# Attention then mixer on one core: 128-row blocks of keys, 23 pairs by DMA transposes, another seed

## The chip, the core and the metric

The kernel runs on one core of a Trainium2 chip. A core has a matrix engine (TensorE, PE in the profile, with its weight loads as PEld), a vector engine (VectorE, DVE), a scalar engine (ScalarE, ACT), a general engine (GpSimd, POOL) and an engine that here issues all DMAs (SyncE, SP). They run side by side and meet through semaphores. The metric is the device time of one execution in microseconds; lower is better. Before the change it is 1030.91 us, the median of three runs (1030.42 to 1031.17).

## The reference

Eight batches of eight heads, 576 positions, 64 channels a head. Attention is causal by blocks of 64 positions; its output is mixed along the sequence with two thin matrices and along the channels with a two-layer network.

```python
def _attn_ref(q, k, v):
    scores = scale * np.matmul(q, k.transpose(0, 1, 3, 2))
    mask = block_i >= block_j                  # blocks of 64 positions
    scores = np.where(mask, scores, -1000000000.0)
    scores = scores - np.max(scores, axis=-1, keepdims=True)
    attn = np.exp(scores)
    attn = attn / (np.sum(attn, axis=-1, keepdims=True) + 1e-09)
    return np.matmul(attn, v)

def _moe_ref(x, U, V, w_ch1, w_ch2):           # x: (8, 576, 512)
    h = x.transpose(0, 2, 1) @ U @ V           # U: (576, 32), V: (32, 576)
    u = x + h.transpose(0, 2, 1)
    ch = np.maximum(u @ w_ch1, 0.0) @ w_ch2    # 512 -> 2048 -> 512
    return u + ch
```

## The kernel before

The 64 heads are worked on in 32 pairs, four pairs to a batch. The 576 queries of a head fall into five tiles: tile 0 has the first 64 queries, and tile i has queries 128 i - 64 to 128 i + 64. Because of the mask tile i needs the first 128 i + 64 keys: i whole blocks of 128 keys and one odd block of 64.

For each pair `scores` multiplies q and k on TensorE (line 1323) in two sets, VectorE takes the maxima (line 1351), and ScalarE the exponentials (line 1362). One set's PSUM banks must be read before the next set's scores start. What follows has two forms. Up to pair 10 the probabilities stay in 32 bits: GpSimd divides them (line 1383), TensorE transposes them (line 1537), ScalarE and VectorE copy the transposes out of PSUM (lines 1508 and 1510), and `apply_v` multiplies them with v in 32 bits (line 1558). The pairs in `XP`, 11 to 31, split each probability into two 16-bit halves (`halve`, lines 1413 to 1440). The DMA engines transpose the halves, four transposes to a pair, issued by SyncE (line 1449), and `apply_x` multiplies them with the two halves of v (line 1487): three products of 16-bit halves for each block.

In `apply_x` the transposed blocks of tiles 0, 3 and 4 lie in one set of buffers (the profile calls them pw or spare) and those of tiles 1 and 2 in another (turn). From pair 24 on there is one set of the first for one pair; before, there are two. The columns of tile 4 are rotated by 64, so that its odd block shares a block of 128 rows with the odd blocks of tiles 0 and 3. In that block v has zeros in rows 0 to 63. The odd blocks of tiles 1 and 2 are followed by zeros, written once at the start (memsets after line 1200, columns 320 to 383 and 576 to 639 of the second buffer). The products go in two groups with a PSUM bank each: group 1 (tiles 3, 4), then group 0 (tiles 0, 1, 2). Odd blocks are read with 64 rows but for tile 4's, which is read with 128. ScalarE moves each bank out (line 1502), and `mix` takes the result through U and V (lines 1587 to 1667) and writes u to DRAM.

Each batch then has two chunks of 288 tokens in the mixer's first half (`ffn_chunk`, lines 763 and 788, chunks 0 to 15), which needs the scale of the whole batch. The second half (`block_products`, line 1012) runs after the attention, since its buffers take the attention's place. Its weights are prepared by ScalarE, VectorE and GpSimd (line 865, among others).

The order of the work is made when the program is built: a planner simulates the five engines with a cost for each task, and gives an engine that is free the ready task of the lowest priority number. Attention tasks have numbers up to 64,000; the mixer's products on TensorE have 1,000,000 and more, so they fill holes. `VARIANT` is the seed of a disturbance of up to 2% either way on every planned cost. SyncE, too, works in the planned order.

Of the kernel before, what the change touches and what calls it, by code (L numbers as in the profile page):

```python
# [18 lines left out]
P = 128  # L19
# [39 lines left out]
INTO = {"PE": 355, "DVE": 60, "ACT": 60, "POOL": 200, "SP": 60}  # L59
NEAR, DL, PORT = 130, 3000, 200  # L60
MOVES, AHEAD, LAND = 400, 1500, 2000
VARIANT = 50
PEQ = 1450.0
PVX = 150.0
NF = 6
# [11 lines left out]
KP = 1  # L77
START = {"PE": 4400, "DVE": 3100, "ACT": 2400, "POOL": 2700, "SP": 700}
SPL = 5
XP = tuple(range(11, 32))  # L80
SLOTS = (8, 5)
XS, XD, MOVE = 1400.0, 3500, 3000
XG = (2, 3)
# [114 lines left out]
class Plan:  # L198
# [8 lines left out]
    def add(self, engine, ns, prio, fn, reads=(), writes=(), hold=(), after=0, port=False, move=410):  # L207

        n = len(self.tasks)
        ns *= 1 + 0.04 * ((n * 40503 + 7919 * VARIANT) % 65536 / 65536 - 0.5)  # L210
        deps = set()
        for b in reads:
            deps.update(b.writers)
            if b.pool is not None:
                deps.update(m for m in b.readers if self.tasks[m][0] != engine)
            b.readers.append(n)
        for b in hold:
            deps.update(b.readers, b.writers)
        for b in writes:
            deps.update(b.readers, b.writers)  # L220
            b.writers, b.readers = [n], []
        deps.discard(n)
        slots = [b for b in dict.fromkeys((*reads, *writes)) if b.pool is not None]
        for b in slots:
            b.users += 1
        self.tasks.append((engine, ns, prio, fn, deps, after, slots, port or engine == "POOL", move))
# [116 lines left out]
def attention_then_mixer(  # L343
# [32 lines left out]
    def buf(pool, shape, dtype, name):  # L376
        return Buf(pool.tile(shape, dtype, name=name))
# [29 lines left out]
    def take(r, name):  # L407
        n = used[name] = used.get(name, -1) + 1
        return r[n % len(r)]
# [68 lines left out]
    def largest(src, n, buf, mu, i, prio):  # L478

        add(  # L480
            "DVE", _dve(n), prio,
            lambda: nc.vector.tensor_reduce(out=mu[:, i : i + 1], in_=src(), op=ALU.max, axis=AX.X, apply_absolute_value=True), [buf], [mu.parts[i]],
        )
# [36 lines left out]
    def power_of(mu, sc, prio, pool):  # L520

        row, ba = take(row_r[1], "rowv"), Buf(pool=pool)
        add(
            "PE", 115, prio,
            lambda: nc.tensor.transpose(out=ba[:, 0:P], in_=mu[:, 0:1].to_broadcast([P, P]), identity=factor["ident"].ap),
            [mu.parts[0]], [ba],
        )

        def exponent():
            x = row[:, 0:1]  # L530
            nc.vector.tensor_reduce(out=x, in_=ba[:, 0:P], op=ALU.max, axis=AX.X)
            nc.vector.tensor_scalar(out=x, in0=x, scalar1=TINY, scalar2=2.0 ** -22, op0=ALU.max, op1=ALU.mult)
            for n, op in enumerate((ALU.bitwise_xor, ALU.bitwise_and)):
                last = nc.vector.tensor_scalar(
                    out=sc[:, n : n + 1].bitcast(I32), in0=x.bitcast(I32), scalar1=EXPONENT, scalar2=EXPONENT,
                    op0=ALU.bitwise_and, op1=op,
                )
            return last

        add("DVE", 730, prio, exponent, [ba], [row, sc])  # L540
# [658 lines left out]
    def turn_of(h, g):  # L1199
        if g:  # L1200
            x = turn_lo[h // 2 % 2][h % 2]
            return x[:, : 2 * SLOTS[1], :], [x]
        x = pw_of(h)[1]
        return x.ap.bitcast(F16)[:, : 2 * SLOTS[0] * P].rearrange("p (a q) -> p a q", q=P), x.parts

    vh = buf(ep, [P, 10, D], F16, "vh")
# [72 lines left out]
    def load_v(p, pr):  # L1279
# [5 lines left out]
        )  # L1285
        if p in XP:
            add("POOL", 250, pr, lambda: nc.gpsimd.memset(raw[0:64, 4:10:5, :], 0.0), [], [raw])

    def job(p):

        if p in XP:
            return ((0, 4), (1, 3), (0, 0), (0, 1), (1, 2))
# [4 lines left out]
    def scores(p, s, pr):  # L1297
# [8 lines left out]
        def view(i):  # L1306
            rows, w = P if i else 64, P * i + 64
            if i == 4:
                return wide[:, :, :T]
            if i > 1:  # L1310
                return pair[i - 2][:, :w]
            return wide[:rows, side[i][0], side[i][1] : side[i][1] + w]

        def products(mine):

            def block(x, n, k0=0, k1=None):
                r = slice(64 * x, 64 * x + 64)
                i, c = (n + 1) // 2, 64 * (n > 0 and n % 2 == 0)
                k1 = 64 * (n + 1) if k1 is None else k1
                at = (k0 + 64) % S if i == 4 and p in XP else k0  # L1320
                o = view(i)[c : c + 64]
                o = o[:, at // T, at % T : at % T + k1 - k0] if i == 4 else o[:, k0:k1]
                nc.tensor.matmul(o, raw[r, 64 * n : 64 * n + 64], raw[r, S + k0 : S + k1], start=True, stop=True)  # L1323

            for x in mine:
                block(*x)
# [7 lines left out]
        else:  # L1334
            if p == XP[0] and not s:
                add("DVE", 130, pr, lambda: nc.vector.memset(wide[0:64, 0, 0:64], NEG), [raw], [wide], hold=[before[-2]])
# [3 lines left out]
                lambda: products((  # L1340
                    *(last if p in XP else ((a, 7, 0, T), (a, 8, 0, T), (b, 5), (b, 6), (a, 7, T, 512), (a, 8, T, S))),
                    (b, 3), (b, 4), (a, 1), (a, 2), (a, 0),
# [110 lines left out]
    def apply_x(p, pr):  # L1453
        xt, vr = xt_r[p % 2], vr_r[p % 2]
        vl = vr.ap.rearrange("p a b -> p (a b)").bitcast(F16).rearrange("p (a b x) -> p a b x", b=D, x=2)[:, :, :, 0]
        turned = [[turn_of(2 * p + s, g) for g in range(2)] for s in range(2)]
        sc, mu = take(vs_r, "vs"), take(mv_r, "mv")
        largest(lambda: vr.ap.rearrange("p a b -> p (a b)"), 10 * D, vr, mu, 0, pr)
        power_of(mu, sc, pr, banks_p(p))
        iv = sc[:, 1:2]  # L1460
        add(
            "POOL", 145 + 0.85 * 10 * D, pr,
            lambda: nc.gpsimd.tensor_scalar(
                out=vr.ap, in0=vr.ap, scalar1=sc[:, 0:1], scalar2=2.0 ** -16, op0=ALU.mult, op1=ALU.mult
            ),
            [sc], [vr],
        )
        add("ACT", _act(10 * D, True), pr, lambda: nc.scalar.copy(vh.ap, vr.ap), [vr], [vh])
        add("POOL", 60 + 2.2 * 10 * D, pr, lambda: nc.gpsimd.tensor_sub(vl, vr.ap, vh.ap), [vh], [vr])
        bank = [Buf(pool=banks_p(p)) for _ in range(2)]  # L1470
        n = [QS[g + 1] - QS[g] for g in range(2)]
        whole = [vh, vr, *(b for r in turned for _, x in r for b in x)]
        order = Buf()

        def products(g):
            for i in ((0, 1, 2), (3, 4))[g]:
                t, at, _ = slot_of[i]
                own, at = i in (3, 2), -(-at // P)
                half = 3 if i == 4 else at + i
                ops = [(j, v, a) for j in range(i + 1) for v, a in ((vh.ap, 0), (vl, 0), (vh.ap, 1))]  # L1480
                for m, (j, v, a) in enumerate(ops):
                    w = P if j < i else 64
                    x = max(P * i + 64 - QS[g] - w, 0)
                    o = 64 if i and w == 64 else 0
                    r = slice(0, P if j < i or i == 4 else 64)
                    for s in range(2):
                        nc.tensor.matmul(  # L1487
                            bank[g][64 * s : 64 * s + 64, x : x + w], v[r, 5 * s + j, :],
                            turned[s ^ own][t][0][r, SLOTS[t] * a + (at + j if j < i else half), o : o + w],
                            start=m == 0, stop=m == len(ops) - 1,  # L1490
                        )

        for g in (1, 0):
            cost = 3 * sum(2 * i + 4 + 0.425 * (P * i + 64) for i in ((0, 1, 2), (3, 4))[g])
            add(
                "PE", cost + PVX * g, pr if g else -1e5, lambda g=g: products(g), [*whole, *([] if g else [order])],
                [bank[g], *([order] if g else [])], hold=xt.parts,
            )
        for g in (1, 0):
            add(  # L1500
                "ACT", _act(n[g]) + 105, pr,
                lambda g=g: nc.scalar.activation(xt[:, QS[g] : QS[g + 1]], bank[g][:, : n[g]], AF.Copy, scale=iv),
                [bank[g], sc], [xt.parts[g]],
            )
# [185 lines left out]
    for p in range(NH // 2):  # L1690
        pr = 2000.0 * p
        if p + 1 < NH // 2:
            load_qk(p + 1, max(pr - LA, 1.0))
        for s in range(2):
            scores(p, s, pr + 10 + 20 * s - (SL if p < NPAIR else SL2))
            (halve if p in XP else normalise)(p, s, pr + 30)
        if p in XP:
# [75 lines left out]
```

## Time and profile before

| | |
|---|---|
| median of three runs | 1030.91 us |
| the profiled execution | 1030.43 us |
| its span, first to last instruction | 1028.6 us |
| TensorE busy | 1017.1 us, 99% |
| VectorE, ScalarE, GpSimd busy | 850.2, 678.6, 408.1 us |
| mean granted clock of TensorE | 0.999 |

Busy time is the union of an engine's instructions. Matmuls overlap each other, and their ends are modelled, so what a matmul costs is read from the start of one to the start of the next. Idle time of an engine is given with what ended it. The first products of `apply_x` stand at 215 us, the last end at 608 us, and the second half of the mixer has TensorE alone from 698 us.

### The profile page before, as it was taken

How to read it: one execution, taken by the hardware profiler on the slowest of the kernel's cores; microseconds unless marked ns; L12 is line 12 of the kernel's file. 1: busy time of each engine (PE TensorE's matmuls, PEld its weight loads, DVE VectorE, ACT ScalarE, POOL GpSimd, SP SyncE). 2: the span in 40 equal slices, each digit the busy share in tenths (PEclk: the TensorE clock that was granted, in tenths of full speed). 3: DMA queues.
4: the chain of work that ended last, by engine and by line, in shares of the span. 5: the costliest groups of instructions: out<-in, count | busy, mean ns of one | idle time of the engine just before them, and what ended most of it. 6: DMA issues, size and time to landing. Idle time of an engine off the chain costs nothing.

```text
span 1028.6 us, 27187 instructions
## 1 busy us (share of the span) xinstructions
PE 1017.1 (99%) x10505; PEld 807.1 (78%) x10505; DVE 850.2 (83%) x1834; ACT 678.6 (66%) x1721; POOL 408.1 (40%) x649
## 2 busy tenths in 40 slices
PE   9999999999999999999999999999999999999998
PEld 7667787787877888778888887777777777777776
DVE  5789999878788788787888746427999999999998
ACT  6889779887877887987777655414545454555453
POOL 4745453756747666666666647600000000000000
PEclk9999999999999999999999999999999999999999
DMA  4544663698998989997998734111314224133121
GB/s 135 173 139 150 182 199 90 187 219 171 204 219 191 208 202 190 213 225 176 225 198 174 146 95 148 46 52 38 105 41 134 69 71 139 35 105 105 39 89 47
DMA packets 210738, 143.28 MB, mean 139 GB/s; under 512 B 149360, under 2 KB 193392, under 8 KB 210608
## 3 DMA queue, kind: packets, MB, share of 16 engines
q1 hardware_dynamic: 210608, 141.54, 56.6%
q8 instruction: 82, 1.34, 0.5%
q14 instruction: 48, 0.39, 0.1%
HBM read 76.23 MB, written 29.49 MB: 103 GB/s over the span
## 4 chain that ended last, share of the span: by engine, by line
PE 93%; ACT 4%; DVE 2%; POOL 1%; issue 0%; ACTq 0%; POOLq 0%; DVEq 0%
PE bb L1012 32%; PE bf L788 18%; PE bf L763 17%; PE ba L1487 6%; PE bw L1323 5%; PE bq L1323 3%; PE ba L1558 3%; PE ba L1590 2%; PE ba L1537 2%; PE ba L1616 1%; ACT p L1362 1%; PE ba L1644 1%; PE bf L1731 1%; POOL p L1383 0%; PE bf L1537 0%
## 5 line engine op out<-in xcount | busy, mean ns | idle before, releaser
L788 PE MATMUL bf<-hh,w2h 128*128 128x288 f16 x512 | 146.8, 287 | 0.4 <-DVE ot L800 0.2
L788 PE MATMUL bf<-hl,w2h 128*128 128x288 f16 x512 | 146.4, 286 | 0.0
L788 PE MATMUL bf<-hh,w2l 128*128 128x288 f16 x512 | 146.4, 286 | 0.0
L788 PEld LDWEIGHTS <-w2h 128*128 128x128 f16 x1024 | 100.2, 98 | 26.1 <-issue 1.7
L763 PEld LDWEIGHTS <-w1h 128*128 128x128 f16 x1024 | 99.2, 98 | 26.9 <-issue 2.9
L1012 PE MATMUL bb<-ph,w1h 128*128 128x288 f16 x448 | 118.9, 286 | 0.0
L1012 PE MATMUL bb<-ph,w1l 128*128 128x288 f16 x448 | 118.9, 286 | 0.0
L1012 PE MATMUL bb<-ph,w2h 128*128 128x288 f16 x448 | 118.9, 286 | 0.0
L1012 PE MATMUL bb<-ph,w2l 128*128 128x288 f16 x448 | 118.9, 286 | 0.0
L1012 PEld LDWEIGHTS <-w1h 128*128 128x128 f16 x896 | 87.7, 98 | 22.2
L1012 PEld LDWEIGHTS <-w2h 128*128 128x128 f16 x896 | 87.7, 98 | 22.2
L1362 ACT ACTIVATE p<-bw,mx 128x192 f32<-128x192 f32 (+2 forms) x192 | 92.2, 485 | 18.9 <-DVE mx L1351 16.9
L1351 DVE TENSOR_REDUCE mx<-bw 128x1 f32<-128x192 f32 (+2 forms) x192 | 78.2, 433 | 30.4 <-PE bw L1323 29.8
L934 ACT CAST ph<-hb 128x576 f16<-128x576 f32 x96 | 63.6, 666 | 54.6 <-PE bb L1012 33.2
L1323 PE MATMUL bw<-raw 64*64 64x192 f32 (+4 forms) x980 | 97.4, 330 | 0.3 <-ACT p L1362 0.2
L771 DVE SCALAR_TENSOR_TENSOR hl<-bf,hh 128x288 f16<-128x288 f32 x128 | 57.8, 453 | 45.7 <-ACT hh L768 44.5
L763 PE MATMUL bf<-uh,w1l 128*128 128x288 f16 x512 | 92.7, 287 | 0.0
L1012 PE MATMUL bb<-pl,w2h 128*128 128x288 f16 x448 | 91.5, 286 | 0.0
L1012 PE MATMUL bb<-pl,w1h 128*128 128x288 f16 x448 | 91.5, 286 | 0.0
L1323 PE MATMUL bq<-raw 64*64 64x384 f32 (+1 forms) x496 | 89.3, 469 | 0.2 <-POOL raw L1273 0.2
L1432 POOL TENSOR_TENSOR hl<-p,hl 128x448 f16<-128x448 f32 (+1 forms) x84 | 75.9, 914 | 28.8 <-ACT hl L1431 9.5
L763 PE MATMUL bf<-uh,w1h 128*128 128x288 f16 x512 | 83.8, 286 | 1.5 <-DVE hl L771 1.0
(227 smaller groups left out, 2692.8 us busy)
## 6 DMA issues: line engine op xcount, KB each, us to landing
raw<-in_qk_dram SPq DMA_DIRECT2D x31, 576.0 KB, 4.6
st<-in_w_dram SPq DMA_DIRECT2D x24, 512.0 KB, 4.3
o_d<-ot SPq DMA_DIRECT2D x72, 144.0 KB, 2.2
vr<-in_v_dram SPq DMA_DIRECT2D x32, 320.0 KB, 3.6
ur<-u_d SPq DMA_DIRECT2D x64, 144.0 KB, 2.8
wr<-o_d SPq DMA_DIRECT2D x32, 288.0 KB, 3.0
out_dram<-wr SPq DMA_DIRECT2D x31, 288.0 KB, 2.3
u_d<-ut SPq DMA_DIRECT2D x28, 288.0 KB, 3.0
```

The costliest lines, as they stand in the source:

```text
L763: nc.tensor.matmul(ps[:, :T], w()[wn][:, k, fs], m[k].ap, start=(i == 0), stop=(i == len(ops) - 1))
L771: lambda ps=ps, th=th, tl=tl: nc.vector.scalar_tensor_tensor(out=tl.ap, in0=ps[:, :T], scalar=0.0, in1=th.ap, op0=ALU.max, op1=ALU.subtract),
L788: nc.tensor.matmul(ps[:, :T], w()[wn][:, f, ms], hs[f][x].ap, start=(i == 0), stop=(i == len(ops) - 1))
L934: add("ACT", _act(n * T, True), E, lambda: nc.scalar.copy(h.ap[:, :n, :], x[0]()), [x[1]], [h])
L1012: nc.tensor.matmul(bank[:, i, :T], x()[:, w(k)], p.ap[:, k, :], start=first and n == 0, stop=last and n == len(ops) - 1)
L1323: nc.tensor.matmul(o, raw[r, 64 * n : 64 * n + 64], raw[r, S + k0 : S + k1], start=True, stop=True)
L1351: lambda i=i, n=n: nc.vector.tensor_reduce(out=mx[: P if i else 64, n : n + 1], in_=view(i), op=ALU.max, axis=AX.XY if i == 4 else AX.X, n ...
L1362: return nc.scalar.activation(out.rearrange("p (j k) -> p j k", j=2) if i == 4 else out, view(i), AF.Exp, bias=mx[:rows, n : n + 1], accum ...
L1432: add("POOL", 60 + 2.2 * w, pr, lambda hi=hi, lo=lo, x=x: nc.gpsimd.tensor_sub(lo, x, hi), [pt, *to], to)
L1487: nc.tensor.matmul(bank[g][64 * s : 64 * s + 64, x : x + w], v[r, 5 * s + j, :], turned[s ^ own][t][0][r, SLOTS[t] * a + (at + j if j < i ...
L1537: nc.tensor.transpose(out=to, in_=pt_r[i][h % PB[i]][:, j * P : (j + 1) * P], identity=perm.ap)
L1558: nc.tensor.matmul(bank[g][64 * s : 64 * s + 64, x : n[g]], vr[:, 5 * s + j, :], pw[g][s][:, _at(g, j)], start=(j == 0), stop=(j == NK[g] ...
```

## The change

Five edits. Odd blocks are read with 128 rows, but for tile 3's own, which keeps 64. The groups change places: tiles 0, 1, 2 come first and tiles 4, 3 second, with tile 3 last; the dependence that orders the two groups and the copies out of PSUM are turned round with them. `XP` begins with pair 9, so pairs 9 to 31 take the path of `halve` and `apply_x`. The seed goes from 50 to 11. A list is renamed.

```diff
-VARIANT = 50
+VARIANT = 11
-XP = tuple(range(11, 32))
+XP = tuple(range(9, 32))
@@ apply_x
         def products(g):
-            for i in ((0, 1, 2), (3, 4))[g]:
+            for i in ((0, 1, 2), (4, 3))[g]:
                 t, at, _ = slot_of[i]
                 own, at = i in (3, 2), -(-at // P)
                 half = 3 if i == 4 else at + i
-                ops = [(j, v, a) for j in range(i + 1) for v, a in ((vh.ap, 0), (vl, 0), (vh.ap, 1))]
-                for m, (j, v, a) in enumerate(ops):
+                some = [(j, v, a) for j in range(i + 1) for v, a in ((vh.ap, 0), (vl, 0), (vh.ap, 1))]
+                for m, (j, v, a) in enumerate(some):
...
-                    r = slice(0, P if j < i or i == 4 else 64)
+                    r = slice(0, 64 if i == j == 3 else P)
...
-                            start=m == 0, stop=m == len(ops) - 1,
+                            start=m == 0, stop=m == len(some) - 1,
...
-        for g in (1, 0):
+        for g in (0, 1):
             cost = 3 * sum(2 * i + 4 + 0.425 * (P * i + 64) for i in ((0, 1, 2), (3, 4))[g])
             add(
-                "PE", cost + PVX * g, pr if g else -1e5, lambda g=g: products(g), [*whole, *([] if g else [order])],
-                [bank[g], *([order] if g else [])], hold=xt.parts,
+                "PE", cost + PVX * g, -1e5 if g else pr, lambda g=g: products(g), [*whole, *([order] if g else [])],
+                [bank[g], *([] if g else [order])], hold=xt.parts,
             )
-        for g in (1, 0):
+        for g in (0, 1):
             add(
                 "ACT", _act(n[g]) + 105, pr,
```

## Rows read from the trace of the kernel before

**Rows 1.** The page, part 1: engine, busy us (share of the span), instructions.
```profile
PE 1017.1 (99%) x10505; PEld 807.1 (78%) x10505; DVE 850.2 (83%) x1834; ACT 678.6 (66%) x1721; POOL 408.1 (40%) x649
```

**Rows 2.** Windows: stretch and length, busy PE, PEld, DVE, ACT, POOL; clock, DMA share, GB/s.
```profile
130.00:180.00 50.00, 48.23 (x469) 38.19 (x467) 46.62 (x126) 41.92 (x117) 21.97 (x42) 1.00 0.46 140
215.00:608.00 393.00, 392.17 (x5062) 315.17 (x5061) 312.55 (x809) 304.00 (x885) 248.25 (x390) 1.00 0.91 195
608.00:648.50 40.50, 40.23 (x341) 32.31 (x338) 23.16 (x43) 21.15 (x38) 28.78 (x24) 1.00 0.39 117
698.50:1028.60 330.10, 326.35 (x2665) 260.44 (x2662) 316.25 (x457) 164.94 (x249) 0.00 (x0) 1.00 0.27 78
```

**Rows 3.** Timeline of TensorE in one product: start us, us, engine, line, operands, count.
```profile
215.52 0.22 PE L1487 MATMUL ba<-pw,vr 128*64 128x128 f16 x2
...
215.69 0.22 PE L1487 MATMUL ba<-pw,vr 128*64 128x128 f16 x2
215.74 0.37 PE L1487 MATMUL ba<-pw,vh 128*64 128x128 f16 x4
215.95 0.20 PE L1487 MATMUL ba<-pw,vr 64*64 64x64 f16 x2
...
216.18 0.22 PE L1487 MATMUL ba<-pw,vr 128*64 128x128 f16 x2
...
216.74 0.25 PE L1487 MATMUL ba<-pw,vh 128*64 128x128 f16 x4
216.83 0.20 PE L1487 MATMUL ba<-pw,vr 128*64 128x64 f16 x2
```

**Rows 4.** The chain that ended last, around the attention's end: start us, us, what.
```profile
605.19 3.09 PE ba L1487 x90
...
636.77 11.76 PE bf L788 x96
648.53 0.73 PE bf L763 x6
```

**Rows 5.** Timeline of a pair by 32-bit transposes; then windows of line 1537 alone.
```profile
163.26 2.94 PE L1558 MATMUL ba<-spare,vr 128*64 128x256 f32 x32
...
168.32 0.60 PE L1537 MATMUL ba<-ident,p 128*128 128x128 f32 x4
168.76 0.41 PE L763 MATMUL bf<-uh,w1l 128*128 128x288 f16 x2
...
0.00:1028.60 1028.60, 41.35 (x286) 31.99 (x286) 1.00 0.57 139
```

**Rows 6.** Timelines of VectorE, GpSimd, ScalarE after the attention.
```profile
628.38 0.27 DVE L516 TENSOR_SCALAR sc<-rowu 128x2 f32<-128x2 f32 x1
...
629.87 0.51 POOL L741 TENSOR_SCALAR us<-ur,sc 128x288 f32<-128x288 f32 x1 [1.25 <-DVE wr L865]
...
646.55 0.43 ACT L746 CAST uh<-us 128x288 f16<-128x288 f32 x1 [2.23 <-POOL us L741]
```

**Rows 7.** Timeline: a product's start, and the next pair's first DMA transpose.
```profile
586.17 0.25 PE L1487 MATMUL ba<-pw,vh 128*64 128x128 f16 x2
...
588.19 2.79 SPq L1449 DMA_TRANSPOSE pw<-hl  x1
```

**Rows 8.** Timeline: a set's last exponential, a product, the next set's scores.
```profile
256.16 0.20 ACT L1362 ACTIVATION_READ_ACCUMULATOR p<-bq,mx 128x1 f32 x1
...
256.70 0.25 PE L1487 MATMUL ba<-pw,vh 128*64 128x128 f16 x2
...
259.60 0.41 PE L1323 MATMUL bw<-raw 64*64 64x224 f32 x2
```

**Rows 9.** Groups of instructions, shapes apart: busy us, mean ns, idle before.
```profile
L1440 DVE SCALAR_TENSOR_TENSOR hl<-p,rv,hl 128x576 f16<-128x576 f32 x42 | 35.4, 844 | 3.3 <-ACT hl L1435 2.2 <-DMA st<-in_w_dram 0.9
```

**Rows 10.** Timeline of TensorE: two consecutive products' starts.
```profile
441.03 0.25 PE L1487 MATMUL ba<-pw,vh 128*64 128x128 f16 x2
...
475.84 0.25 PE L1487 MATMUL ba<-pw,vh 128*64 128x128 f16 x2
```

## The prediction

> **What bounds the kernel now.** I first read the engine table. TensorE is busy for 1017.1 of 1028.6 us [rows 1], so the question is what fills it. The windows [rows 2] say so stage by stage. From 215 to 608 us, the attention of the pairs that use DMA transposes, TensorE is busy 392.17 of 393 us, while VectorE has 312.55, ScalarE 304.00 and the DMA engines 0.91. In the last 330 us it is busy 326.35. The granted clock is 1.00 throughout. TensorE never waits because the mixer's products (lines 763 and 788) rank behind all attention work and fill every hole. Two things follow. Less work on TensorE in the attention stage moves mixer work forward, whoever paces the attention. But mixer work can only move as far as its inputs are ready, and the last batch's inputs depend on the end of the attention. So two numbers decide: the TensorE work removed, and the room ahead of the first product that needs the last pairs.
>
> **Odd blocks on 128 rows.** A timeline of one product [rows 3] shows the price of the 64-row blocks. In steady state three steps of 128 rows by 128 columns (a step is two matmuls side by side) take 0.17 us (215.52 to 215.69), 0.056 us each. From 215.74 to 216.18 stand the last 128-row step, the three 64-row steps of tile 3's odd block, and the first 128-row step of tile 4: 0.44 us. Two steps of 0.056 off leave 0.33 us for the three. Tile 4's odd block has 128 rows already: from 216.74 to 216.83, 0.09 us pass for one 0.056 us step and one 64-column step, so that one costs about 0.03 us and three cost 0.09. A visit to 64 rows therefore costs 0.33 - 0.09 = 0.24 us more than the same block at 128 rows; going in and coming back take it, not columns. The product visits 64 rows four times (tiles 3, 0, 1, 2) and would do so once, at its end, where it leaves a 64-row block now too. So 3 x 0.24 = 0.72 us go, and a product of 3.09 us [rows 4] becomes 2.37. Over 21 pairs that is 15.1 us. Bounds: nothing, if what costs is the diagonal block's place and not its rows (against that stands tile 4's block), and 0.33 x 3 x 21 = 20.8 us.
>
> The Trainium skill ("TensorEngine Tiling (Array Packing)", Key Properties) says that changing the tiling mode drains TensorE; the rows agree that it costs. Its page "TensorE: Matmul & The Clock Gate" puts a drain at about 128 cycles, which is an estimated 53 ns at 2.4 GHz, so six changes would be worth 0.32 us a product and 6.7 us in all; the rows show more than twice that, and I go by the rows.
>
> **Pairs 9 and 10 by DMA transposes.** A pair on the old path needs 26 fp32 transposes on TensorE (286 over eleven pairs). Four take 0.44 us from start to start (168.32 to 168.76), 0.11 each; all of them have 41.35 us of busy time, 0.145 each [rows 5]. So 2.9 to 3.8 us, and I take 3.3. Its fp32 product takes 2.94 with its tail, 2.9 without. Both go and one product of 2.37 comes, with one small transpose of at most 0.15: 3.3 + 2.9 - 2.5 = 3.7 us a pair (3.3 to 4.2), 7.4 us for two. The scores stay. Together TensorE loses 15.1 + 7.4 = 22.5 us.
>
> The other engines gain work: two splits a pair in VectorE's longest form at 0.84 us each [rows 9], with the shorter forms, the largest value of v and less the copies that go, at most about 4 us a pair on VectorE; something alike on ScalarE and GpSimd; and eight transposes in SyncE's queue. This falls where VectorE is busy 46.62 of 50 us and the DMA engines are 0.46 busy (130 to 180 us) [rows 2]. The weights of the mixer share that stretch with a lower rank, so they can give way; bounds 0 to 8 us of delay for the attention, and I take 0. What is queued behind these transposes on SyncE are the next pair's q, k and v and the stores of mixer results; the former are fetched a pair ahead.
>
> **Swapped groups, and the seed.** The product's order becomes tiles 0, 1, 2, then 4, then 3. One release moves. From pair 24 on one set of tiles holds the transposed blocks of tiles 0, 3 and 4, so the next pair's transposes into them wait for their last read. Now that is tile 0's, 2.02 us after the product starts (586.17 to 588.19) [rows 7]. Afterwards it is tile 3's, at 2.37: 0.35 us later, seven times, 0 to 2.4 us on the attention; I take 1. The seed shifts every planned cost by up to 2% either way and so reorders all engines. It adds no work. Its price is a scatter of the attention's end, and I read its size off the spacing of products: 34.8 us between 441.03 and 475.84 [rows 10], against a mean of 18.5 over the seven that follow (475.84 to 605.19). Such delays come and are partly made up, so I allow 6 us either way.
>
> In the other direction, scores queue behind a product on TensorE. ScalarE's last exponential of a set ends at 256.36, a product starts at 256.70, and the next scores start at 259.60 [rows 8]. That happens before nine of 37 score sets after 212 us. Nine times 0.72 is 6.5 us, the most by which the attention could gain; other engines fill part of such holes, so I take 3. The sum for the attention's end is -3 + 1 + 0 = -2 us, bounds -6.5 to +10.4, before the seed's scatter.
>
> **What is late next.** The chain [rows 4] gives the room. The last product of the attention ends at 608.28; the first product of mixer chunk 14, the first that needs the last batch, is at 648.53. TensorE works 40.23 of 40.5 us between [rows 2], on work whose inputs are ready. Take 22.5 us out ahead of it and that work is done near 626. But chunk 14 needs the scale of the last batch, written at 628.65, and then four scaled and split tiles of it. In this run the first scaling starts at 629.87 and the last half-precision tile is done at 646.98 [rows 6], unhurried, for chunk 13 reads the same tiles until 636.77. The shortest chain is 628.65 + 4 x 0.51 + 0.43 = 631.1. After the tiles came free the four took 10.2 us; started at 630 without that wait, but among the weight halves on GpSimd, I put the end at 636.5 (631 to 641). The products of the last stage (line 1012) cannot cover the gap: they first run at 649 here, and their buffers and inputs also wait for the attention's end. So TensorE, full for 390 us, would idle from 626 to 636.5, and of 22.5 us only 648.5 - 636.5 = 12 pass, plus the 2 us by which the attention ends earlier: 14 us. The profiled execution took 1030.43 (1.8 us around its span), so 1016.4; the median of the runs is 0.5 above it, so 1016.9.
>
> **Rivals.** (a) *All of it passes.* If the attention ends some 10 us earlier, or chunk 14's tiles come by 631 and the attention 5 us earlier, the room suffices: 1030.9 - 22.5 = 1008.4. For it speaks that the end is a chain of few waits and not a full engine (ScalarE 304 and GpSimd 248 of 393 us); against it, that the planner must happen on such an order. (b) *The 64-row price does not go*, being that of the corner blocks. Then only 7.4 us go, less than the room, and all pass: 1023.5. Tile 4's block speaks against it. (c) *The attention ends late and takes the place of TensorE as the bound.* From chunk 14 on the work is fixed, so each microsecond of a later end counts once the room is used up. One more hole like the one from 441 to 476 us, 34.8 - 18.5 = 16.3 us, after pair 24 where one set of tiles leaves no slack, gives -12 + 16.3 = +4.3: 1035.2. It decides from a delay of 12 us. For it speak the DMA engines at 0.91, to which two pairs are added; against it that their stretch is at 0.46. (d) The removed time is eaten to the last: a delay of 10 to 14 us, no change.
>
> By the page's drain price alone TensorE would lose 6.7 + 7.4 = 14.1 us, within what passes here, so the time would again be near 1017.
>
> **Chances.** The forecast, part of the gain lost to the attention's end, has 0.68; its own range, with the end from -8 to +5 us, is 1011 to 1024. (a) 0.20, (b) 0.04, (c) 0.05, (d) 0.03. Half of (a) lies above 1008, and with the edge of (b) the range 1008 to 1025 holds 8 in 10. The measurement can tell a change above 0.2%, about 2 us: faster 0.92, within it 0.03, slower 0.05.
>
> **What would show it.** Right: products of 2.3 to 2.5 us with one 64-row visit; 23 of them; 234 transposes on line 1537 instead of 286; TensorE's busy time down by 20 to 24 us; a new idle stretch of 5 to 15 us shortly after 620 us, ended by the splits of chunk 14 or the last stage's first pieces. Wrong: products that keep 0.1 us gaps at blocks of 128 rows (then the row count was not the cause), no idle after 620 (then the room was larger than I read), or idle before 600 us, where mixer chunks would have run out.

## The result, and the profile after

The changed kernel takes 1015.06 us (median; runs from 1013.28 to 1016.42), the kernel before 1030.67 beside it. The ratio is 0.9847 [0.983, 0.9864]: 15.6 us less. The forecast was 1016.9. Two executions far slower than their neighbours (3623.59 us with the seed alone, 1148.51 with more dummy matmuls) are left out of the medians below.

The engine table of the changed kernel, against [rows 1]:

```profile
span 1014.5 us, 27280 instructions
...
PE 998.3 (98%) x10547; PEld 794.7 (78%) x10547; DVE 852.1 (84%) x1848; ACT 685.2 (68%) x1731; POOL 415.1 (41%) x651
```

TensorE's busy time falls by 18.8 us, the span by 14.1. The difference is idle time. The profiled execution is the longest of the four runs (1016.42), so its 14.0 us are less than the medians' 15.6. The end of one product shows what became of the 64-row visits (columns as in [rows 3]):

```profile
196.83 0.20 PE L1487 MATMUL ba<-pw,vr 128*64 128x64 f16 x2
196.86 0.26 PE L1487 MATMUL ba<-pw,vh 128*64 128x64 f16 x4
196.96 0.22 PE L1487 MATMUL ba<-pw,vr 128*64 128x128 f16 x2
...
197.35 0.37 PE L1487 MATMUL ba<-pw,vh 128*64 128x128 f16 x4
197.55 0.20 PE L1487 MATMUL ba<-pw,vr 64*64 64x64 f16 x2
197.58 0.20 PE L1487 MATMUL ba<-pw,vh 64*64 64x64 f16 x2
197.71 0.30 PE L763 MATMUL bf<-uh,w1h 128*128 128x288 f16 x1
```

One visit to 64 rows is left, the last block. Behind it stands the step to the mixer's full array: 197.58 to 197.71, 0.13 us where a step inside the visit takes 0.03. Where a mixer product follows, the whole product takes 2.39 us, as in the next fence, against 3.09 in [rows 4].

The chain of waits around the attention's end:

```profile
600.95 2.39 PE ba L1487 x90
...
622.59 11.76 PE bf L788 x96
634.35 0.73 PE bf L763 x6
```

The scale of the last batch in VectorE's timeline (start, us, engine, line, operands):

```profile
623.44 0.41 DVE L516 TENSOR_SCALAR sc<-rowu 128x2 f32<-128x2 f32 x1
```

The last half-precision tiles for chunk 14 in ScalarE's timeline:

```profile
630.83 0.75 ACT L746 CAST uh<-us 128x288 f16<-128x288 f32 x2
```

The last product ends at 603.34 (600.95 + 2.39), 4.9 us earlier than before; the tiles are complete at 631.58, 28.2 us later, as estimated; chunk 14 starts at 634.35, 14.2 us earlier. So 2.8 us of room are left and nothing idles. The windows of the changed kernel, by stage as in [rows 2], and of the first 215 us:

```profile
0.00:215.00 215.00, 202.65 (x2005) 153.11 (x2007) 177.13 (x489) 172.09 (x510) 112.66 (x213) 0.99 0.58 163
160.00:200.00 40.00, 35.02 (x407) 27.13 (x406) 35.58 (x104) 33.57 (x88) 20.48 (x34) 1.00 0.76 170
215.00:603.30 388.30, 388.28 (x5224) 316.16 (x5217) 319.23 (x836) 311.42 (x911) 261.85 (x408) 1.00 0.98 205
603.30:634.30 31.00, 31.00 (x262) 25.07 (x259) 17.95 (x38) 21.79 (x35) 20.43 (x15) 1.00 0.41 123
```

The first two windows in the kernel before:

```profile
0.00:215.00 215.00, 208.36 (x2038) 159.22 (x2039) 181.47 (x497) 174.72 (x524) 115.02 (x222) 1.00 0.54 159
160.00:200.00 40.00, 38.43 (x379) 30.79 (x380) 35.20 (x98) 36.31 (x103) 20.58 (x41) 1.00 0.48 142
```

After 215 us TensorE is full through the attention's end. The new idle time lies ahead of it: 12.35 us (215 less 202.65) against 6.64, and of the 5.7 us more, 3.4 lie between 160 and 200 us. There VectorE is busy 35.58 of 40 us and the DMA share has risen from 0.48 to 0.76; VectorE's load alone doesn't explain it, since it was 35.20 us before. TensorE's longest waits in the first 215 us (engine, line and producer; total us, times, longest):

```profile
PE bf L788 <- DVE hl L771: 3.0, 2, 2.5
PE bf L1155 <- DVE hl L1143: 1.6, 1, 1.6
PE bf L788 <- DVE ot L800: 1.6, 2, 1.4
```

The first and the third are mixer work whose VectorE input came late; the second stands in the kernel before with the same 1.6 us. Behind the longest wait, 2.5 us until 178.10, stands ScalarE: the chain of waits runs there through the rescaling of weights that ScalarE does just ahead of the hidden tile (line 768) from which VectorE makes `hl`:

```profile
172.97 1.97 ACT w2h L619 x2
174.96 2.18 ACT w2l L619 x2
```

ScalarE and VectorE are both busy through the whole of that wait (2.50 of 2.50 us), so the wait alone doesn't say that VectorE is the limit.

### The profile page after: what moved, and what is told of

Same layout as the page of the kernel before. It is cut to its first block, busy times and chain, and to the rows that moved or that the text cites. A ratio compares the mean times of both kernels' runs of the same rounds, so it can differ in the third digit from the quotient of the medians.

```text
span 1014.5 us, 27280 instructions
## 1 busy us (share of the span) xinstructions
PE 998.3 (98%) x10547; PEld 794.7 (78%) x10547; DVE 852.1 (84%) x1848; ACT 685.2 (68%) x1731; POOL 415.1 (41%) x651
## 4 chain that ended last, share of the span: by engine, by line
PE 89%; ACT 5%; DVE 4%; DMA 1%; issue 0%; POOL 0%; DVEq 0%; ACTq 0%; SPq 0%
PE bb L1012 32%; PE bf L788 17%; PE bf L763 17%; PE bw L1323 6%; PE ba L1487 5%; PE bq L1323 3%; ACT p L1362 2%; PE ba L1590 2%; PE ba L1616 1%; PE ba L1558 1%; PE ba L1537 1%; DMA st<-in_w_dram 1%; DVE mx L1351 1%; PE ba L1644 1%; PE bf L1558 1%; DVE z L435 1%
## 5 line engine op out<-in xcount | busy, mean ns | idle before, releaser
L1432 POOL TENSOR_TENSOR hl<-p,hl 128x448 f16<-128x448 f32 (+1 forms) x92 | 83.4, 914 | 38.7 <-ACT hl L1431 11.6
L1323 PE MATMUL bw<-raw 64*64 64x288 f32 (+4 forms) x988 | 97.5, 329 | 1.1 <-issue 0.8
L763 PE MATMUL bf<-uh,w1l 128*128 128x288 f16 x512 | 89.9, 286 | 0.0
L1323 PEld LDWEIGHTS bw<-raw 64*64 64x64 f32 x988 | 71.7, 133 | 19.9 <-issue 4.8
```

Of the source, the lines that this page charges most:

```text
L763: nc.tensor.matmul(ps[:, :T], w()[wn][:, k, fs], m[k].ap, start=(i == 0), stop=(i == len(ops) - 1))
L1432: add("POOL", 60 + 2.2 * w, pr, lambda hi=hi, lo=lo, x=x: nc.gpsimd.tensor_sub(lo, x, hi), [pt, *to], to)
```

## The experiments

**The rows alone.** On the kernel before, with the order of groups, the pairs and the seed left:

```diff
-                    r = slice(0, P if j < i or i == 4 else 64)
+                    r = slice(0, 64 if i == j == 3 else P)
```


> The kernel before with one edit: odd blocks on 128 rows but for tile 3's own. The planned costs are the same, so the order of the work is the one of before. If the row count is what costs, the product falls from 3.04 us (63.82 us over 21 pairs) to about 2.39, the length it has after the change, and TensorE loses 21 x 0.65 = 13.7 us. Theory R (room: chunk 14 of the mixer cannot start earlier than some 28 us after the attention's last product, here 608.3 + 28 = 636.5, against 648.5 now) lets 12 us pass, a little more if the shorter products also end the attention earlier: 1017 to 1019 us. Theory W (every microsecond of TensorE work is a microsecond of time) gives 1030.7 - 13.7 = 1017.0. Rival B (the price belongs to the place of the diagonal block and not to its rows) gives no change, 1030 to 1031, and products that stay above 3.0 us.

1018.97 us, 0.9892 [0.9876, 0.9909]. The end of a product in its timeline:

```profile
216.55 0.20 PE L1487 MATMUL ba<-turn,vr 128*64 128x64 f16 x2
216.58 0.20 PE L1487 MATMUL ba<-turn,vh 128*64 128x64 f16 x2
216.71 0.42 PE L763 MATMUL bf<-uh,w1l 128*128 128x288 f16 x2
```

Its chain of waits around the attention's end:

```profile
593.79 2.50 PE ba L1487 x90
...
624.78 11.76 PE bf L788 x96
636.53 0.73 PE bf L763 x6
```

Its window over the attention (columns as in [rows 2]):

```profile
215.00:596.30 381.30, 380.47 (x5048) 309.96 (x5043) 312.18 (x806) 301.57 (x882) 246.98 (x389) 1.00 0.93 200
```

A product takes 2.50 us. Its end leaves a tile of 128 rows by 64 columns, and the same 0.13 us pass before the mixer's first matmul. So the price is one of each change of tile shape, the one to the full array too, and not of 64 rows: eight changes a product before, three here, two in the changed kernel (the one on entry, which all have, not counted). 0.59 over five is 0.118 us each, and six are 0.71. Why a change costs this much, a drain or weight loads that no longer run ahead, the runs don't tell apart.

The other finding is how the saving passes. The last product's end moves by 12.0 us (608.28 to 596.29), chunk 14's start by 12.0 (648.53 to 636.53) and the span by 12.0 (1028.6 to 1016.6). All three move as one: the instructions of each engine stand in the same order as before, and TensorE hardly waits.

**The rows back.** The changed kernel with the old row line:

```diff
-                    r = slice(0, 64 if i == j == 3 else P)
+                    r = slice(0, P if j < i or i == 4 else 64)
```


> The changed kernel with the row counts of before (64 rows for the odd blocks of tiles 0 to 3); groups, pairs 9 and 10 and seed as changed, so the order of the work is that of the changed kernel. If rows are what costs, the product returns from 2.39 to 3.0 to 3.1 us, 23 x 0.65 to 0.7 = 15 to 16 us more TensorE work, and the room ahead of chunk 14 is not used up at all, so all of it shows: 1029 to 1032 us by both W and R. Rival B: 1014 to 1016, as the changed kernel.

1027.74 us, 0.9973 [0.9964, 0.9982]: the row line is worth 12.7 us here and 11.4 above. Its chain:

```profile
610.78 2.97 PE ba L1487 x90
...
633.00 11.76 PE bf L788 x96
644.76 0.73 PE bf L763 x6
```

That is below the 1029 us expected, since line 1487 takes 13.8 us more by starts and not 15. A whole product takes 2.97: with tiles 0, 1, 2 first it has seven changes of shape, and 2.39 + 5 x 0.118 is 2.98. The last one ends 10.4 us later than in the changed kernel (613.75), and chunk 14 starts 10.4 us later: again both as one.

**The pairs back.** The changed kernel with pairs 9 and 10 on the old path:

```diff
-XP = tuple(range(9, 32))
+XP = tuple(range(11, 32))
```


> The changed kernel with pairs 9 and 10 back on 32-bit transposes by TensorE. By the two traces those two pairs cost TensorE 52 transposes and 64 products, 10.9 us less 1.7 us of a stretch at half clock, and save two products of 2.39: 9.2 - 4.8 = about 4.4 us more work on TensorE. Theory I (the two pairs on the new path leave TensorE short of mixer work before 203 us, where it idles 5.5 us after the change and 1.8 before) expects that idle to go back to about 2 us, so that the two pairs are worth 0 to 2 us: 1013 to 1017. The rival (their idle comes from the seed's order and not from the pairs) expects idle to stay at 5 us and the time at 1019 to 1020.

1024.09 us, 0.9933 [0.9914, 0.9951]. The two pairs are worth 9.0 us here, more than either reading expected. TensorE's busy time is 1007.5 us, 9.2 more than in the changed kernel; 1.7 of that comes from the clock, which stands at half for 6.8 us (83.7 to 90.5) here and for 3.4 in the changed kernel. Before 215 us TensorE already idles 10.0 us without the two pairs, as the window of that stretch has it:

```profile
0.00:215.00 215.00, 204.99 (x1949) 153.72 (x1949) 177.29 (x484) 165.96 (x500) 107.53 (x214) 0.98 0.50 155
```

**More work out of the products.** To tell whether the room at the attention's end limits the gain, the changed kernel leaves out the products with the low half of v:

```diff
-                some = [(j, v, a) for j in range(i + 1) for v, a in ((vh.ap, 0), (vl, 0), (vh.ap, 1))]
+                some = [(j, v, a) for j in range(i + 1) for v, a in ((vh.ap, 0), (vh.ap, 1))]
```


> The changed kernel without the products of the low half of v in the 16-bit path (the middle one of three products of each block): it leaves out that part of the computation, and takes about a third of 23 products of 2.39 us from TensorE, 17 to 18 us, with the planned order unchanged. Theory W: 1015.1 - 17.5 = 997 to 998 us, no new idle time. Theory R: after the change the last tiles of chunk 14 are ready at 631.6 us and its first product starts at 634.3, so some 3 us of room are left, plus what the attention's end gains from shorter products (0 to 5 us): 1007 to 1012 us, with 8 to 15 us of idle time on TensorE between 605 and 635.

1005.52 us, 0.9758 [0.9743, 0.9773]: 9.5 us below the changed kernel by the medians, 11.6 by the spans (1014.5 to 1002.9). Its chain at chunk 14:

```profile
611.13 11.76 PE bf L788 x96
622.89 0.73 PE bf L763 x6
```

Its window where the idle stretch was expected:

```profile
605.00:635.00 30.00, 30.00 (x247) 23.92 (x245) 18.67 (x37) 14.81 (x28) 21.44 (x18) 1.00 0.43 134
```

The time lies between the two theories, 1.5 us below the range of the room and 7.5 above that of the other. The idle stretch that the room asked for is absent: from 605 to 635 us TensorE is full. The last product ends 12.1 us earlier (591.2), chunk 14 starts 11.5 earlier. The room did not act here, and that theory falls by its own mark. Line 1487 lost 16.3 us by starts; 11.6 pass. Some 2 of the missing 5 are idle time in small pieces; the rest is spread over other lines' spacing and stays open.

**The seed.** The changed kernel with the seed of before, the kernel before with the new one, and the changed kernel with a third:

```diff
-VARIANT = 11
+VARIANT = 50
```


> The changed kernel with the seed of before, 50. Rows alone gave 11.4 us and pairs 9 and 10, under seed 11, about 9; together more than the change gives (15.4). Theory S (the new seed's order costs several us: after the change TensorE idles 12.4 us before 215 us, 6.6 before the change, and its clock is at half for 3.4 us) expects 1007 to 1011 us, less idle time before 215 us and no stretch at half clock. Theory I (the idle time comes with pairs 9 and 10 on the new path) expects idle to stay at 10 to 12 us and the time at 1013 to 1017.

```diff
-VARIANT = 50
+VARIANT = 11
```


> The kernel before with the seed of after, 11, and nothing else. Theory S: 1034 to 1038 us, with 10 us or more of idle time before 215 us. Theory I: 1029 to 1032, idle near 7 us.

```diff
-VARIANT = 11
+VARIANT = 12
```


> The changed kernel with a third seed, 12, to see how far seeds scatter. TensorE's work stays at 996 to 999 us; the time follows its idle time, 8 to 20 us by seed: 1008 to 1020 us. If the attention's end were the bound and not TensorE, time and TensorE's busy plus idle before 215 us would not move together.

1017.75 us, 0.9874 [0.9859, 0.9889]; 1034.83, 1.004 [1.0026, 1.0054]; 1028.68, 0.9981 [0.9971, 0.999]. On the kernel before seed 11 costs 4.5 us, on the changed one it gains 2.7 (the intervals of the two ratios just overlap), and seed 12 gives back 13.6. The seed alone came out as theory S had it, with 11.2 us of idle time before 215 us. The seed of before left 10.9 us of idle time, as theory I had it, at a time that neither had. So the seed and the pairs each bring idle time. Seed 12 missed its expectation in time and in TensorE's work, 1002.7 us. The window of the first 215 us with seed 12:

```profile
0.00:215.00 215.00, 199.03 (x1994) 150.16 (x1997) 174.37 (x479) 170.28 (x505) 108.30 (x208) 0.99 0.54 158
```

TensorE idles 16.0 us there, the most of all runs, and its longest waits in that stretch are for another producer, scores behind ScalarE's exponentials:

```profile
PE bw L1323 <- ACT p L1362: 3.0, 4, 2.1
PE bq L1323 <- ACT p L1362: 2.7, 2, 2.3
```

**Rows and groups, and pair 10 alone,** both with the seed of before:

```diff
-VARIANT = 11
-XP = tuple(range(9, 32))
+VARIANT = 50
+XP = tuple(range(11, 32))
```


> Rows and swapped groups without the other edits: seed 50, pairs 11 to 31. With rows alone a product takes 52.86 / 21 = 2.52 us, since its one visit to 64 rows lies inside; after the change it takes 2.39, with the visit at the end. If that is all that the groups do, TensorE loses 21 x 0.13 = 2.7 us more than with rows alone: 1016 to 1017 us. If the new order of the groups upsets the plan, 1018 to 1024, with more idle time.

```diff
-VARIANT = 11
-XP = tuple(range(9, 32))
+VARIANT = 50
+XP = tuple(range(10, 32))
```


> The changed kernel with seed 50 and pair 10 alone on the new path (pairs 10 to 31). From pair 11: 1019.3 us, busy 1004.9 and idle 9.0; from pair 9: 1017.75, busy 998.4 and idle 13.5, of which a half-clock stretch of 3.4 us adds some 1.7 to busy. If idle grows with the pairs because mixer work is not ready before about 200 us, one pair gives up less: busy 1001 to 1002, idle 9 to 11, time 1015.5 to 1018. If idle is a matter of the order alone, anything from 1012 to 1022.

1019.28 us, 0.9888 [0.9873, 0.9902], and 1017.59, 0.9875 [0.9861, 0.989]. The first is the case in which the new order of the groups upsets the plan; the second came as expected. So by the seed of before: rows -11.4 (1018.97), groups nothing (1019.28), pair 10 -1.7 (1017.59), pair 9 nothing (1017.75), seed 11 -2.7 (1015.06). Of these steps only the rows stand clear of the intervals of the ratios. Where pair 9's gain went is seen in the engine table and in the window of the first 215 us. The engine table with pair 10 alone:

```profile
PE 1001.6 (99%) x10542; PEld 797.6 (78%) x10542; DVE 848.9 (84%) x1841; ACT 683.1 (67%) x1726; POOL 408.5 (40%) x650
```

Its window:

```profile
0.00:215.00 215.00, 208.56 (x2095) 159.97 (x2096) 182.61 (x501) 175.09 (x517) 114.14 (x218) 1.00 0.56 164
```

The engine table with both pairs:

```profile
PE 998.4 (98%) x10579; PEld 795.4 (78%) x10579; DVE 854.9 (84%) x1848; ACT 682.9 (67%) x1731; POOL 411.0 (40%) x651
```

Its window:

```profile
0.00:215.00 215.00, 204.12 (x2101) 155.30 (x2103) 180.64 (x498) 173.72 (x514) 112.86 (x213) 0.99 0.59 165
```

Pair 9 takes 3.2 us of work from TensorE, and TensorE idles 4.4 us more before 215 us (10.9 against 6.4). VectorE gains 6.0 us by pair 9, but only 3.7 by both pairs: without them it is busy 851.2 us.

**The weights earlier.** If the idle time came from late weight halves, a higher rank for them would remove it (priority number 11,000 instead of 14,000), tried under both seeds:

```diff
-WP4 = 14000.0
+WP4 = 11000.0
```


> The changed kernel with the second half of the mixer's first weights one and a half pairs earlier in rank (priority 11000 instead of 14000). With pairs 9 and 10 on the new path TensorE idles 5.0 us between 160 and 200 us, longest while mixer products wait for the hidden tile's low half (2.5 us) and for results to be moved out (1.4). Theory P (those weights and the splits behind them come late by their rank): idle in 160 to 200 us falls to about 1 to 2 us, time by 2 to 4 us: 1011 to 1013. Theory V (VectorE is the bound there, 35.6 of 40 us busy, so earlier weights only push attention back): idle moves, time 1014 to 1018.

> The same edit with seed 50, against 1017.75 us for the changed kernel with seed 50, where TensorE idles 5.2 us between 160 and 200 us, 2.6 of them waiting for the low halves of those very weights. Theory P: 1013 to 1015, without those waits. Theory V: 1016 to 1021.

1019.67 us, 0.9893 [0.9878, 0.9907], and 1019.68, 0.9899 [0.9878, 0.9921]: no gain, 4.6 and 1.9 us more than without; the first lies above both theories. Under seed 11 the idle time before 215 us is 13.0 us, and much of it is one wait of the mixer for VectorE, beside a stretch at half the clock. TensorE's timeline, with the idle time ahead in brackets:

```profile
163.34 0.40 PE L788 MATMUL bf<-hh,w2h 128*128 128x288 f16 x1 [4.66 <-DVE hl L771]
```

The windows of that wait and of the stretch around its end (the granted clock is third from the end):

```profile
158.70:163.34 4.64, 0.00 (x1) 0.00 (x1) 4.01 (x11) 4.64 (x7) 0.56 (x2) 0.77 0.24 80
161.20:168.00 6.80, 4.66 (x28) 3.55 (x31) 4.49 (x10) 5.65 (x14) 1.94 (x5) 0.50 0.24 77
```

What is done earlier for the weights is missing for the hidden tiles: through the wait ScalarE is busy all of 4.64 us, with the weights' halves and their rescaling (lines 573 and 619) and then the hidden tile, and VectorE 4.01. Theory P falls. That VectorE is the limit, as theory V has it, isn't shown either: here ScalarE stands in front of it, and its order was not tried by itself. Under seed 50 the idle time from 160 to 200 us falls from 5.2 to 2.1 us, as theory P asked, and yet no time is gained, since TensorE is busy 4.9 us longer; 1.7 of these come from a stretch at half the clock of 6.8 us where there were 3.4.

**Dummy matmuls for longer.** The planner fills holes of TensorE with dummy matmuls (line 1731) in the first 130 us of its plan. With seed 50, up to 210:

```diff
-WARM = 130e3
+WARM = 210e3
```


> The changed kernel with seed 50, in which the planner goes on filling idle time of TensorE with small unused products up to 210 us of its own time instead of 130 (150 more of them, by its plan between 150 and 205 us, where TensorE idled 5 us and its clock then stood at half for 3.4 us). Theory C (the half-clock stretch follows from that idling and costs some 1.7 us): no half-clock stretch, less idle time, 1015.5 to 1016.5 against 1017.75. Rival: the small products stand in front of attention work that would have come sooner, 150 at 0.056 us is 8.4 us for some 6 us of idle, so 1018 to 1021, with or without the half-clock stretch.

1018.59 us, 0.9886 [0.9866, 0.9906], against 1017.75 without, as the rival had it. With seed 50 the clock had fallen to half from 176.3 to 179.7 us; here it has not. The window with the dummies up to 130:

```profile
176.30:179.70 3.40, 3.40 (x15) 2.17 (x16) 2.79 (x9) 3.40 (x4) 0.59 (x1) 0.50 0.28 113
```

The same window with them up to 210:

```profile
176.30:179.70 3.40, 3.40 (x53) 3.17 (x51) 3.40 (x9) 3.40 (x5) 0.00 (x0) 1.00 0.23 93
```

Its engine table:

```profile
PE 1004.2 (99%) x10729; PEld 803.6 (79%) x10729; DVE 854.9 (84%) x1848; ACT 683.1 (67%) x1731; POOL 411.3 (40%) x651
```

TensorE is busy 5.8 us longer and idles 4.7 less before 215 us, and the span is 1016.3 against 1015.8. The holes are filled and nothing comes earlier. No version that computes everything beat the changed kernel.

## Why the prediction was right or wrong

**What bounds the kernel now.** Right from 215 us on: TensorE is busy 388.28 of 388.30 us there until the last product ends. Before 215 us mixer work doesn't fill every hole: TensorE idles 6.64 us there in the kernel before and 12.35 in the changed one.

**Odd blocks on 128 rows.** Right in mechanism and near in size. From start to start a product loses 0.70 us (predicted 0.72): 3.09 to 2.39 where mixer work follows, 2.9 to 2.2 where scores follow, which run in 64-row tiles too and spare the last change. Over 21 products line 1487 loses 13.7 us (63.8/21 less 54.9/23, times 21) for the predicted 15.1: fewer products are followed by scores now (five of 23, nine of 21 before), and four are split by other work between their groups, at 0.91 + 1.60 us, one change more. The working called the price one of 64 rows; the rows-alone run shows that it belongs to each change of shape, the one to the full array too. The drain that the Trainium skill names ("TensorEngine Tiling (Array Packing)", Key Properties) fits that; 0.118 us a change is over twice the 53 ns estimated from "TensorE: Matmul & The Clock Gate" (Step-by-step: what each phase is for).

**Pairs 9 and 10.** Right in count (23 products, 234 transposes) and in TensorE's work, but the other engines' part, taken as 0, was the term that failed here. The windows of line 1537 alone, against [rows 5]:

```profile
0.00:1014.50 1014.50, 33.73 (x234) 26.28 (x234) 1.00 0.61 145
```

By starts the transposes lose 6.8 us and the 32-bit products 4.1, and two products of 2.4 come: 6.1 for the predicted 7.4, of which a half clock took some 1.7. It fell here (window; clock third from the end):

```profile
85.30:88.70 3.40, 3.40 (x24) 2.12 (x22) 2.75 (x7) 2.18 (x6) 2.14 (x5) 0.50 0.19 66
```

The prediction let the mixer's weights give way in the stretch where VectorE is busy 46.62 of 50 us. Their rescaling on ScalarE (line 619) doesn't give way: its priority number is -1, and it stands ahead of the hidden tile in the longest wait. By the waits for split hidden tiles, TensorE then lacked work for its holes: by seed 50 the two pairs give 1.5 us of their 6.5 us of busy time. By seed 11 they give 9.0, because TensorE idles 10 us before 215 us there without them. The idle time before 215 us, with rows and groups changed, is 6.8 us without pairs and seed, 10.0 with the seed, 10.9 with the pairs and 12.35 with both: the two delays overlap in part and don't add. Which engine sets them isn't shown; no run takes ScalarE's or VectorE's part alone.

**Swapped groups, and the seed.** The groups: nothing that could be told (1018.97 and 1019.28). Line 1487 loses another 2.8 us by them, and the spacing of other lines takes as much (763: 1.1, 1590: 0.8, 1644: 0.6), with 1.3 us of idle time on top. The scatter of the seed was under-sized: against seed 50 the changed kernel takes -2.7 us with seed 11 and +10.9 with seed 12, for 6 either way. It lies in TensorE's work and idle time, the latter mostly before 215 us, and not at the attention's end alone. The attention's end moved by -4.9 us, not -2, and for another reason.

**What is late next.** This is the step that failed. It held the attention's end nearly still and let only the filling work between it and chunk 14 move ahead. But that filling work stands in a fixed order between the attention's own instructions on TensorE, so with TensorE full the attention moves forward with all else: by 12.0 us in the rows-alone run, by 12.1 in the run without the low half. In the changed kernel, whose order is a new one, chunk 14 starts 14.2 us earlier by both ways: 4.9 come from the attention's end, and 9.3 from filling work that now stands ahead of that end, so that 31.0 us lie between the two instead of 40.2. The tiles' delay of 28.2 us behind the last product was estimated right, and 2.8 us of room remained; in no run does chunk 14 start less than 28 us behind the last product, so the room as such isn't refuted. The idle stretch after 620 us does not exist, and idle time ahead of 600 us grew: two of the prediction's own signs of being wrong.

**The sum.** It was right by cancellation, which is luck. Forecast: 22.5 us of TensorE work removed, 10.5 lost at the attention's end, 2 from its earlier end: 14. Measured in the profiled runs: 18.8 removed, 4.7 lost to idling (5.7 more before 215 us, some 1 less behind): 14.1 of span. The removed work was 3.7 us short: products 1.4, pairs 1.3, other lines (spacing up 2.8, dummies down 1.8) 1.0.

**Rivals.** (a), all passes: its mechanism held after 215 us, and its 1008.4 was missed for the idling ahead and the smaller removal. (b), the price stays, falls with the products' 2.39 us. (c), the attention ends late, did not come, though seed 12 shows that a disturbed order can take nearly all of the gain: against the changed kernel TensorE is busy 4.4 us longer, idles 3.6 us more before 215 us and 3.5 more behind. (d), no change, did not come by seed 11; by seed 12 the change is 0.2%.

## What to carry to other kernels

Count TensorE's changes of tile shape, the one to the next full-array matmul among them, and place small tiles beside a change that must come anyway: six changes fewer were worth 0.71 us a product. Five of the six came by the rows; the sixth, by the order of the groups, didn't show in the time. Where each engine's order is fixed and the bounding engine is full, work taken out of it moves what stands behind it as one, so a wait further on moves too and must not be held still in the estimate (12.0 us at three places in one run; in another 11.6 of 16.3 us passed). Work handed to other engines is priced in the stretch where it falls: here VectorE and ScalarE were busy 35.20 and 36.31 of 40 us there, and two pairs gave 1.5 us or 9.0, by the order around them.

## What the runs showed of the hardware that was not expected

The granted clock fell to 0.50 (1.2 of 2.4 GHz) for 3.4 us in several orders, and for 6.8 us with the weights early and with the pairs back. With seed 50 it fell behind a mixer matmul that had waited 1.95 us. TensorE's timeline there; from start to start three matmuls took 0.72 us, 0.24 each, against 0.12 at the full clock:

```profile
175.57 0.30 PE L788 MATMUL bf<-hh,w2l 128*128 128x288 f16 x1 [1.95 <-DVE w2l L577]
...
176.69 0.45 PE L788 MATMUL bf<-hh,w2h 128*128 128x288 f16 x1
...
177.41 0.45 PE L788 MATMUL bf<-hh,w2h 128*128 128x288 f16 x1
...
179.88 0.29 PE L788 MATMUL bf<-hl,w2h 128*128 128x288 f16 x1
180.00 0.29 PE L788 MATMUL bf<-hh,w2h 128*128 128x288 f16 x1
```

So 3.4 us cost about 1.7 us of work. It is a small price beside the idling itself, and the run with more dummies, where the clock doesn't fall, gains nothing; it also has more work, so what removing the fall alone would give isn't shown. Executions of one kernel differ in it: of the four of the changed kernel the one with a mean clock of 1.0 took 1013.28 us, the three at 0.997 and 0.998 took 1014.69 to 1016.42.
